# Softcap attention followed by a four-expert attention layer: stage B by two slots per token instead of four experts, its gate on GpSimd, and one exponential per pair of heads in stage A

## The chip, the cores and the metric

One NeuronCore of a Trainium2 chip runs the whole program. The metric is the device time of one execution in microseconds, the median over runs.

## The reference

`q`, `k` and `v` have shape (8, 12, 448, 64): batch, heads, tokens, head width. Stage A is attention with a soft cap, without a causal mask; stage B gives its output to an attention layer with E = 4 experts of width 64, of which each token uses the two with the largest gate logits.

```python
# stage A
scores = scale * np.matmul(q, k.transpose(0, 1, 3, 2))
scores = cap * np.tanh(scores / cap)
...
attn = np.exp(scores)
attn = attn / (np.sum(attn, axis=-1, keepdims=True) + 1e-09)
...
# stage B: x is stage A's output, (8, 448, 768)
logits = x @ w_gate
topk = np.argpartition(-logits, K, axis=-1)[..., :K]      # K = 2
...                                                       # w: softmax over the two chosen logits
for e in range(E):
    q = x @ wq[e]; k = x @ wk[e]; v = x @ wv[e]
    scores = scale * (q @ k.transpose(0, 2, 1))
    causal = np.triu(np.ones((S, S), dtype=bool), 1)
    ...                                                   # softmax, causal, in a
    ye = a @ v @ wo[e]
    for kk in range(K):
        mask = topk[:, :, kk] == e
        out += mask[..., None] * w[:, :, kk:kk + 1] * ye
```

In stage B every token is a key for every expert; only as a query does it belong to two of them.

## The kernel before, in words

**Stage A** goes over 48 pairs of heads (six pairs, HP, make one batch). GpSimd casts q, k and v of a pair to f16 four pairs ahead (`a_cast`, L241 to L263). TensorE transposes them into one PSUM tile (`a_tr`, L272 to L279), and VectorE copies them out (L289 to L296, L223). The scores of a pair are seven blocks of 128 keys by 448 queries, four for the first head and the tail of both, three for the second. `fill` (L305) computes them in four parts, T0 to T3, of 2, 2, 2 and 1 blocks, each into a tile of `ps_score`, a PSUM pool of two buffers. `tanh` (L318) reads each part on ScalarE; `expo` (L328) then takes the exponential of the first head's four blocks (1792 columns) and of the second's three (1344). `a_pv` (L337 to L369) multiplies with v on TensorE and normalizes on VectorE; `a_xt` (L383) transposes the result into `xT`, stage B's input, with six pairs per batch.

**Stage B** follows each batch while stage A goes on with the next one. `b_qk` (L486) and `b_v` (L395) project q, k, v and the logits from `xT`; two experts (index r, then e = 2r + g) share one 128-row tile of q and k. The k copy on VectorE spreads the two experts over separate columns with zeros in the other half (`b_k_out`, L479), so that `b_fill` (L516) gets one expert's scores, 1024 or 960 columns without the blocks above the diagonal. `b_exp` (L534) takes their exponential on ScalarE and GpSimd sets the diagonal blocks' upper parts to zero (L548). `b_gate` and `b_gate2` (L429, L449) find the two largest logits and their weights in nine small VectorE operations; `b_gexp` (L424) is the gate's exponential on ScalarE. `b_pv` (L553) multiplies with v for one expert and scales rows by weight over sum; `b_ot` (L582) and `b_wo` (L599) make the output. The last batch has no stage A beside it and goes its own way in `last_batch` (L798).

**Order.** The schedule is written by hand. `prog` (L688 to L697) fixes ScalarE's order: for a pair T0, T1, the second exponential of the pair before, T2, T3, the first exponential. In pairs 6(b+1)+3 and, as a rule, two later (`EXPB`, L685), the stage-B exponentials ("X") of batch b for r = 0 and r = 1 are put in, one before and one after the pair-before's exponential. A planner (`Plan`, L16 to L123) places TensorE's other work: each unit has an assumed TensorE and VectorE time, units that it needs, and a due time. `do_fill` (L714) first forces all that the next ScalarE tile needs (`fill_dep`, L711), then lets the planner emit other units until the score buffer is expected to be free, and then emits the fill. Engines run their queues in order, so a unit that waits holds back what is queued behind it. Four PSUM buffers (`ps_aux`) serve all else.

```python
            prog += t[0:2] + x[0:1] + e1 + x[1:2] + t[2:4] + [("E", p, 0)]
```

Of the kernel before, what the change touches and what calls it, by code (L numbers as in the profile page):

```python
# [125 lines left out]
def kernel(  # L126
# [26 lines left out]

    WIN = (0, 128, 256, S - 128)

    const = ctx.enter_context(tc.tile_pool(name="const", bufs=1))
# [158 lines left out]
    y = {}  # L315
    pr = {}

    def tanh(p, i):  # L318
        g = i // 2
        n = len(HALF[i])  # L320
        if i % 2 == 0:
            y[(p, g)] = actp.tile([128, 4 - g, S], f16, name=f"y{g}_{p}", tag=f"y{g}")
        nc.scalar.activation(  # L323
            y[(p, g)][:, 2 * (i % 2) : 2 * (i % 2) + n, :], score.pop((p, i))[:, 0:n, 0:S],
            AF.Tanh, scale=isc / capf,
        )

    def expo(p, g):  # L328
        pt = actp.tile([128, 4 - g, S], f16, name=f"p{g}_{p}", tag=f"p{g}")
        nc.scalar.activation(pt, y.pop((p, g)), AF.Exp, scale=capf)  # L330
        pr[(p, g)] = pt

# [4 lines left out]
    def a_pv_mm(p, i, n, heads):  # L337

        if n == 0 and 0 in heads:
            pvs[p, i] = ps_aux.tile([128, 2, 2, Dh + 1], f32, name=f"pv{i}_{p}", tag="aux")  # L340
        pv = pvs[p, i]
        w = WIN[2 * i + n]
        for g in heads:
            pt = pr[(p, g)]
            if g == 0:
                nc.tensor.matmul(  # L346
                    pv[:, n, :, :], pt[:, KC, w : w + 128], vtz[p % 8], start=(n == 0),
                    stop=False, skip_group_check=True,
                )
            for c in range(KC):  # L350
                nc.tensor.matmul(  # L351
                    pv[:, n, g, :], pt[:, c, w : w + 128], v16[p % 8][:, g, c, :],
                    start=False, stop=(c == KC - 1), skip_group_check=True,
                )

    def a_pv_out(p, i):
        pv = pvs.pop((p, i))
        if i == 0:
            xt[p] = hd.tile([128, 4, 2, Dh], f16, name=f"xk_{p}", tag="xk")
        else:  # L360
            del pr[(p, 0)], pr[(p, 1)]
        rc = hd.tile([128, 2, 2, 1], f32, name=f"rc{i}_{p}", tag="rc")
        nc.vector.reciprocal(rc, pv[:, :, :, Dh : Dh + 1])  # L363
        nc.vector.tensor_tensor(  # L364
            xt[p][:, 2 * i : 2 * i + 2, :, :], pv[:, :, :, 0:Dh],
            rc.broadcast_to((128, 2, 2, Dh)), ALU.mult,
        )
# [27 lines left out]
    def b_v(b, n, i):  # L395
        s = st[b]
        if n == 0 and i == 0:
            s["vall"] = bp.tile([128, KC, E, Dh + 1], f16, name=f"vall_{b}", tag="vall")
            s["lg"] = bp.tile([128, 4, E], f32, name=f"lg_{b}", tag="lg")
            nc.gpsimd.memset(s["vall"][:, :, :, Dh : Dh + 1], 1.0)  # L400
        w = WIN[n]
# [12 lines left out]
        if b < B - 1:  # L414
            nc.vector.tensor_copy(s["lg"][:, n, :], ps[:, E * Dh : E * Dh + E])
        if n < 3:
            evac(s["vall"][:, n, :, 0:Dh], pse, act=(b == B - 1 and n > 0))
        else:
            assert b < 2 or ("pvB", b - 2, E - 1) in plan.done
            vb = vtB[b % 2]  # L420
            nc.vector.tensor_copy(vb[0:64, 0:E:2, 0:Dh], pse[64:128, 0:E:2, :])
            nc.vector.tensor_copy(vb[64:128, 1:E:2, 0:Dh], pse[64:128, 1:E:2, :])
# [26 lines left out]
    def b_gate2(b):  # L449
# [14 lines left out]
        s["wtok"] = wtok  # L464

    def b_qk_mm(b, r, which, ps, j0, j1):
        w2 = wq2 if which == "q" else wk2
# [11 lines left out]
    def b_k_out(b, r, ps, act=False):  # L479
        assert b < 1 or ("X", b - 1, r, 1) in plan.done  # L480
        kk = kzB[r]
        nc.vector.tensor_copy(kk[0:64, 0:S], ps[0:64, :])
        nc.vector.tensor_copy(kk[64:128, S : S + TL], ps[64:128, KM:S])
        evac(kk[64:128, S + TL : 2 * S], ps[64:128, 0:KM], act)

    def b_qk(b, r, which, i):  # L486
# [4 lines left out]
        if i == 2:  # L491
            (b_q_out if which == "q" else b_k_out)(b, r, ps)

# [17 lines left out]

    COL = {(0, 0): 64, (0, 1): 512, (0, 2): 832, (1, 1): 1024, (1, 2): 1344, (1, 0): 1536}
# [19 lines left out]
    def b_exp(b, r, g):  # L534

        assert b < 2 or ("pvB", b - 2, E - 1) in plan.done
        pb = pB[2 * (b % 2) + r]
        n = 1024 - 64 * g
# [14 lines left out]
    def b_pv(b, e):  # L553

        s = st[b]
        r, g = divmod(e, 2)
        pb = pB[2 * (b % 2) + r]
        if g == 0:
            s["osc", r] = bp.tile([128, 4, 2, Dh], f16, name=f"osc_{b}_{r}", tag="osc")
        pv = ps_aux.tile([128, 4, Dh + 1], f32, name=f"pvB_{b}_{e}", tag="aux")  # L560
        for n in range(4):
# [5 lines left out]
            if n == 3:  # L567
                ops.append((0, vtB[b % 2][:, e, :]))
            for i, (o, rhs) in enumerate(ops):
# [83 lines left out]
    kzB = [const.tile([128, 2 * S], f16, name=f"kzB{i}") for i in range(2)]  # L653
    vtB = [const.tile([128, E, Dh + 1], f16, name=f"vtB{i}") for i in range(2)]
    pB = [const.tile([128, 64 + 1984], f16, name=f"pB{i}") for i in range(4)]

    def b_const(i):
        nc.vector.memset(kzB[i], 0.0)
        nc.vector.memset(vtB[i], 0.0)
        nc.vector.memset(vtB[i][0:64, 0:E:2, Dh : Dh + 1], 1.0)  # L660
        nc.vector.memset(vtB[i][64:128, 1:E:2, Dh : Dh + 1], 1.0)
        for t in pB[2 * i : 2 * i + 2]:
            nc.vector.memset(t[:, 0:64], 0.0)

# [19 lines left out]

    EXPB = {HP * (b + 1) + 3 + 2 * r - (b == B - 2) * r: (b, r) for b in range(B - 1) for r in range(2)}  # L685


    prog = []  # L688
    for p in range(NP):
        t = [("T", p, i) for i in range(4)]  # L690
        e1 = [("E", p - 1, 1)] if p else []
        x = [("X", *EXPB[p], g) for g in range(2)] if p in EXPB else []
        prog.append(("S", p))
        if p < NP - 1:
            prog += t[0:2] + x[0:1] + e1 + x[1:2] + t[2:4] + [("E", p, 0)]
        else:
            prog += t + e1 + [("S", NP), ("E", p, 0), ("E", p, 1)]  # L697
    reads = [o for o in prog if o[0] in "TX"]
# [5 lines left out]
    def dur(o):  # L704
        if o[0] == "S":
            return 0.0
        if o[0] == "X":
            return 0.9
        return 0.06 + 0.373 * (4 - o[2] if o[0] == "E" else len(HALF[o[2]]))

    def fill_dep(o):  # L711
        return (("tr", o[1]),) if o[0] == "T" else (("q", o[1], o[2]), ("k", o[1], o[2]))

    def do_fill():  # L714
# [8 lines left out]
        plan.pe = max(plan.pe, rel, *(plan.done[d] for d in fill_dep(o))) + cost  # L723
        fill(*o[1:]) if o[0] == "T" else b_fill(*o[1:])
        plan.done[("f", nfill)] = plan.pe + plan.LAT
# [11 lines left out]
    def slot(p):  # L737
# [14 lines left out]
        if 1 <= p < NP:  # L752
            es = [("E", p - 1, 0), ("E", p - 1, 1)]
            due = nom["S", p + 1]
# [18 lines left out]
    def batch(b):  # L773
        x = ("xt", HP * b + HP - 1)
        t0, t1 = nom["X", b, 0, 0], nom["X", b, 1, 0]
        pace = 1.0 if b < B - 2 else 0.3
        for r, t in enumerate((t0, t1)):
            plan.parts(("q", b, r), 3, 1.13, 0.55, [x], t - 4.0, b_qk, b, r, "q")
            plan.parts(("k", b, r), 3, 1.13, 0.75, [x], t - 4.0, b_qk, b, r, "k")
        for n in range(4):  # L780
            d = [("v", b, n - 1)] if n else [x]
            plan.parts(("v", b, n), 2, 0.66, 0.6, d, t0 + 2.0 * n, b_v, b, n)
        plan.add(("g1", b), 0.0, 1.0, [("v", b, 3)], t1 + 1.0, b_gate, b, aux=None)
        plan.add(("g", b), 0.0, 0.8, [("g1", b), ("G", b)], t1 + 3.0, b_gate2, b, aux=None)
        for e in range(E):
            due = t1 + pace * (6.0 + 3.0 * e)
            d = [("X", b, e // 2, e % 2), ("g", b)] + [("pvB", b, e - 1)] * (e % 2)
            plan.add(("pvB", b, e), 0.46, 0.7, d, due, b_pv, b, e)
            if e % 2:
                plan.add(("oT", b, e // 2), 0.22, 0.35, [("pvB", b, e)], due, b_ot, b, e // 2)  # L790
        for n in range(4):
            for f in range(2):
                i = 2 * n + f
                d = [("oT", b, 1)] if i == 0 else [("wo", b, *divmod(i - 1, 2))]
                due = t1 + pace * (19.0 + 1.5 * i)
                plan.add(("wo", b, n, f), 0.33, 0.5, d, due, b_wo, b, n, f)

# [98 lines left out]

    ngate = 0

    def gate_exp(wait=False):

        nonlocal ngate
        d = plan.done.get(("v", ngate, 3))
        if d is not None and (wait or d <= plan.act):
            b_gexp(ngate)
            plan.act = max(plan.act, d) + 0.1
            plan.done[("G", ngate)] = plan.act + plan.LAT
            ngate += 1

    nread = 0
    for pos, o in enumerate(prog, 1):  # L910
# [3 lines left out]
        if o[0] == "E":  # L914
            plan.act += dur(o)
            expo(*o[1:])
            plan.done[o] = plan.act + plan.LAT
            gate_exp()
            continue
# [6 lines left out]
        else:  # L926
            b_exp(*o[1:])
            gate_exp()
            plan.done[o] = start + dur(o) + plan.LAT + 0.6
# [41 lines left out]
```

The softmax here doesn't subtract the row's maximum and nothing guards it: scores larger than these inputs give would overflow.

## Time and profile before

| | |
|---|---|
| Median of 3 runs | 340.6 us (339.47, 340.60, 344.87) |
| Profiled execution: time, and span from first to last instruction | 341.0 us, 341.0 us |
| From 9.7 to 311.8 us (stage A, with stage B of seven batches) | ScalarE 298.0 us busy of 302.1, TensorE 257.1, VectorE 230.6, GpSimd 157.8 |
| From 311.8 us to the end (the last batch's stage B) | 29.2 us; ScalarE 8.1, TensorE 17.8 |
| Granted TensorE clock | 0.989 |

In the profile PE is TensorE, PEld its weight loads, DVE VectorE, ACT ScalarE, POOL GpSimd. A timeline line has the start and the duration in us, the engine, the source line, the operation, output and inputs by their names with shapes, and in brackets the idle time before it with what ended it. Names: `s` scores of stage A, `y` tanh, `p` its exponential, `pv` products with v, `xk` the normalized output, `tps` and `xtp` transposes, `qps`, `kps`, `vps` projections, `sB` and `pB` scores and exponential of stage B, `wops` and `ob` the output. Durations of consecutive instructions on one engine overlap.

### The profile page before, as it was taken

How to read it: one execution, taken by the hardware profiler on the slowest of the kernel's cores; microseconds unless marked ns; L12 is line 12 of the kernel's file. 1: busy time of each engine (PE TensorE's matmuls, PEld its weight loads, DVE VectorE, ACT ScalarE, POOL GpSimd, SP SyncE). 2: the span in 40 equal slices, each digit the busy share in tenths (PEclk: the TensorE clock that was granted, in tenths of full speed). 3: DMA queues.
4: the chain of work that ended last, by engine and by line, in shares of the span. 5: the costliest groups of instructions: out<-in, count | busy, mean ns of one | idle time of the engine just before them, and what ended most of it. 6: DMA issues, size and time to landing. Idle time of an engine off the chain costs nothing.

```text
span 341.0 us, 8954 instructions
## 1 busy us (share of the span) xinstructions
PE 280.2 (82%) x3295; PEld 190.1 (56%) x3295; DVE 251.1 (74%) x877; ACT 308.4 (90%) x341; POOL 165.2 (48%) x527
## 2 busy tenths in 40 slices
PE   5766669697899789998799879997899789979772
PEld 1344346465457565765576655765576566657441
DVE  2456656378767897869977897889887897788673
ACT  1999999689999999999999999999999999995422
POOL 2889999555806293256707291438506430220130
PEclk9999999799999999999999999999999999999997
DMA  5989999860172915392087606490162001210116
GB/s 160 264 222 244 244 223 241 202 173 3 48 208 72 293 32 171 123 289 71 7 253 211 184 2 187 138 303 24 47 210 72 3 2 46 94 24 2 48 54 226
DMA packets 65148, 46.21 MB, mean 136 GB/s; under 512 B 25872, under 2 KB 61584, under 8 KB 65104
## 3 DMA queue, kind: packets, MB, share of 16 engines
q1 hardware_dynamic: 53712, 43.43, 44.4%
q0 software_dynamic: 10512, 1.58, 7.3%
q10 hardware_dynamic: 880, 0.62, 0.6%
q8 instruction: 26, 0.43, 0.5%
q14 instruction: 18, 0.15, 0.1%
HBM read 36.19 MB, written 11.01 MB: 138 GB/s over the span
## 4 chain that ended last, share of the span: by engine, by line
ACT 85%; PE 6%; DMA 2%; issue 2%; DVE 2%; POOL 1%; ACTq 0%; POOLq 0%
ACT y L323 39%; ACT p L330 37%; ACT pB L540 7%; POOL pB L548 1%; DMA kf<-in_k_dram 1%; PE qkps L469 1%; PE vps L407 1%; PE s L312 1%; DMA out_dram<-ob 1%; PE sB L528 1%; DMA vtf<-in_v_dram 1%; DVE ob L223 1%; PE qps L469 0%; PE pv L351 0%; ACT L223 0%
## 5 line engine op out<-in xcount | busy, mean ns | idle before, releaser
L323 ACT ACTIVATE y<-s 128x896 f16<-128x896 f32 x192 | 152.6, 880 | 1.9 <-PE s L312 1.9
L330 ACT ACTIVATE p<-y 128x1792 f16<-128x1792 f16 x96 | 149.6, 1562 | 0.0
L548 POOL TENSOR_SCALAR_AFFINE_SELECT pB<-pB 128x128 f16<-128x128 f16 (+1 forms) x128 | 31.9, 280 | 142.9 <-ACT pB L540 141.7
L312 PE MATMUL s<-qt,kz 128*128 128x448 f16 x288 | 82.0, 357 | 14.0 <-ACT y L323 6.0
L351 PE MATMUL pv<-v,p 128*128 128x65 f16 x1152 | 66.2, 194 | 1.2 <-ACT p L330 1.0
L351 PEld LDWEIGHTS <-p 128*128 128x128 f16 x1152 | 53.7, 98 | 11.0 <-ACT p L330 2.0
L346 PE MATMUL pv<-vtz,p 128*128 128x130 f16 x192 | 42.0, 220 | 3.1 <-DVE kz L223 3.0
L364 DVE TENSOR_TENSOR xk<-pv,rc 128x256 f16<-128x256 f32 x96 | 40.7, 424 | 3.3
L312 PEld LDWEIGHTS <-kz 128*128 128x128 f16 x288 | 26.2, 98 | 26.4 <-issue 13.1
L223 DVE COPY ob<-wops 128x384 f32<-128x384 f32 (+1 forms) x60 | 33.1, 556 | 9.3 <-PE wops L594 8.5
L540 ACT ACTIVATE pB<-sB 128x1024 f16<-128x1024 f32 (+1 forms) x32 | 31.9, 999 | 2.4 <-PE sB L528 2.4
L223 DVE COPY kz<-tps 64x384 f16<-64x384 f16 x94 | 32.9, 350 | 0.7
L379 PE MATMUL xtp<-perm,xk 128*128 128x128 f16 x144 | 21.0, 223 | 14.4 <-DVE xk L364 14.2
L594 PE MATMUL wops<-wo,oT 128*128 128x384 f16 x128 | 29.8, 325 | 1.7 <-DVE oT L588 1.7
L407 PE MATMUL vps<-wvg,xT 128*128 128x260 f16 (+1 forms) x192 | 30.6, 276 | 0.0
L379 PEld LDWEIGHTS <-xk 128*128 128x128 f16 x192 | 14.6, 98 | 27.3 <-DVE xk L364 19.1
L363 DVE RECIPROCAL rc<-pv 128x4 f32<-128x4 f32 x96 | 17.2, 179 | 16.6 <-PE pv L351 15.4
L241 POOL CAST q<-qf 112x512 f16<-112x512 f32 x46 | 28.2, 613 | 2.0
L289 DVE COPY qt<-tps 128x384 f16<-128x384 f16 x48 | 16.9, 352 | 15.2 <-PE tps L279 14.8
L242 POOL CAST k<-kf 128x384 f16<-128x384 f32 x48 | 24.4, 509 | 5.0 <-DMA kf<-in_k_dram 5.0
L390 DVE COPY xT<-xtp 128x448 f16<-128x448 f16 x48 | 18.6, 388 | 11.2 <-PE xtp L379 10.8
L258 POOL CAST v<-vf 128x384 f16<-128x384 f32 x48 | 24.4, 508 | 3.5 <-DMA vf<-in_v_dram 0.5
(100 smaller groups left out, 500.5 us busy)
## 6 DMA issues: line engine op xcount, KB each, us to landing
qf<-in_q_dram SPq DMA_DIRECT2D x23, 448.0 KB, 5.2
out_dram<-ob SPq DMA_DIRECT2D x24, 384.0 KB, 2.8
kf<-in_k_dram SPq DMA_DIRECT2D x23, 384.0 KB, 5.3
vf<-in_v_dram SPq DMA_DIRECT2D x23, 384.0 KB, 4.6
ktf<-in_k_dram SPq DMA_DIRECT2D x46, 32.0 KB, 4.7
vtf<-in_v_dram SPq DMA_DIRECT2D x46, 32.0 KB, 4.1
out_dram<-ob SPq DMA_DIRECT2D x7, 192.0 KB, 2.8
qf<-in_q_dram ACTq DMA_DIRECT2D x2, 224.0 KB, 4.1
```

What stands on the lines that cost most here:

```text
L223: (nc.scalar.copy if act else nc.vector.tensor_copy)(dst, src)
L312: nc.tensor.matmul(sc[:, o, 0:S], lhsT, qt, start=True, stop=True)
L323: nc.scalar.activation(y[(p, g)][:, 2 * (i % 2) : 2 * (i % 2) + n, :], score.pop((p, i))[:, 0:n, 0:S], AF.Tanh, scale=isc / capf,)
L330: nc.scalar.activation(pt, y.pop((p, g)), AF.Exp, scale=capf)
L346: nc.tensor.matmul(pv[:, n, :, :], pt[:, KC, w : w + 128], vtz[p % 8], start=(n == 0), stop=False, skip_group_check=True,)
L351: nc.tensor.matmul(pv[:, n, g, :], pt[:, c, w : w + 128], v16[p % 8][:, g, c, :], start=False, stop=(c == KC - 1), skip_group_check=True,)
L364: nc.vector.tensor_tensor(xt[p][:, 2 * i : 2 * i + 2, :, :], pv[:, :, :, 0:Dh], rc.broadcast_to((128, 2, 2, Dh)), ALU.mult,)
L379: nc.tensor.transpose(ps[:, 128 * n : 128 * (n + 1)], src(n), first if n < 3 else last)
L407: nc.tensor.matmul(ps, xT[b][:, j, w : w + 128], wvg[:, j, 0:cols], start=(j == 0), stop=(j == NDC - 1),)
L540: nc.scalar.activation(pb[:, o0 : o0 + n], st[b].pop(("sc", r, g))[:, 0:n], AF.Exp, scale=isc)
L548: nc.gpsimd.affine_select(out=blk, in_=blk, compare_op=ALU.is_ge, fill=0.0, base=0, pattern=[[1, n]], channel_multiplier=-1,)
L594: nc.tensor.matmul(ps, st[b]["oT", r][:, w : w + 128], wo2[r][:, f * (D // 2) : (f + 1) * (D // 2)], start=(r == 0), stop=(r == 1),)
```

## The change

Stage B, for all batches but the last, no longer runs four experts but two slots a = 0, 1: a token's first and second chosen expert in the order of their indices. q of the experts that aren't in the slot is set to zero per token, and the scores of a slot are the sum over both 128-row tiles, so that each token meets its own expert's keys. Slot 0 can hold experts 0 to 2 and slot 1 experts 1 to 3; the product with v is made for the three experts at once, and rows are scaled per expert with weights that are zero for the others. There are thus two exponentials of 1024 columns per batch instead of four (two of 1024, two of 960), with a fill of eight matmuls each. The gate (`s_gate`) moves to GpSimd, with powers of e instead of ScalarE's exponential; it makes the masks, which TensorE transposes (`s_mask`). In stage A the two exponentials of a pair become one of 3136 columns (not in the last pair), and `prog` is T0, T1, X, the exponential of the pair before, T2, T3. The last batch keeps its way with four experts.

The diff, cut to its core:

```diff
-    def expo(p, g):
-        pt = actp.tile([128, 4 - g, S], f16, name=f"p{g}_{p}", tag=f"p{g}")
-        nc.scalar.activation(pt, y.pop((p, g)), AF.Exp, scale=capf)
-        pr[(p, g)] = pt
+    def expo(p, k0, k1):
+
+        if k0 == 0:
+            pr[p] = actp.tile([128, 7, S], f16, name=f"p_{p}", tag="p")
+        nc.scalar.activation(
+            pr[p][:, k0:k1, :], y[p][:, k0:k1, :], AF.Exp, scale=capf
+        )
...
+    def s_gate(b):
...
+        ee = t("ee", E)
+        g.tensor_tensor(ee, euler, lg, ALU.pow)
+        df, gt = t("df", E, E), t("gt", E, E)
+        g.tensor_tensor(df, lgj, lgi, ALU.subtract)
+        g.tensor_scalar(gt, df, 0.0, None, ALU.is_gt)
+        for i in range(1, E):
+            g.tensor_scalar(gt[:, :, i, 0:i], df[:, :, i, 0:i], 0.0, None, ALU.is_ge)
+        r2, rank = t("r2", E, 2), t("rank", E, 1)
+        g.tensor_tensor(r2, gt[:, :, :, 0:2], gt[:, :, :, 2:4], ALU.add)
+        g.tensor_tensor(rank, r2[:, :, :, 0:1], r2[:, :, :, 1:2], ALU.add)
+        sel = t("slt", E)
+        g.tensor_scalar(sel, rank.rearrange("p n e o -> p n (e o)"), 1.5, None, ALU.is_lt)
+
+        mk = t("mk", 8, 1, dt=f16)
+        g.memset(mk, 0.0)
...
+        for a in range(2):
+            s["mb", a] = t(f"mb{a}", E, Dh, dt=f16)
+            g.tensor_copy(s["mb", a], mk[:, :, a:8:2, :].broadcast_to((128, 4, E, Dh)))
+
+        g.tensor_tensor(ee, ee, sel, ALU.mult)
...
+        g.tensor_tensor(den, den, minus, ALU.pow)
...
+        plan.done[("G", b)] = plan.pe + 9.0
+
+    def s_mask(b, a):
...
+        ps = ps_aux.tile([128, 2, 512], f16, name=f"mps{a}_{b}", tag="aux")
+        for r in range(2):
+            transpose4(
+                ps[:, r, :],
+                lambda n: mb[:, n, 2 * r : 2 * r + 2, :].rearrange("p e d -> p (e d)"),
+                ident, swap,
+            )
+        qm = bp.tile([128, 2, S], f16, name=f"qm{a}_{b}", tag=f"qm{a}", bufs=1)
+        nc.vector.tensor_tensor(qm, s["qs"], ps[:, :, 0:S], ALU.mult)
...
+    def s_fill(b, a):
+        s = st[b]
+        ks, qm = s["ks"], s["qm", a]
+        sc = ps_score.tile([128, 1024], f32, name=f"sS{a}_{b}", tag="score")
+        for c in (KC, 0, 1, 2):
+            k0, q0 = (S - 128, KM) if c == KC else (128 * c, 128 * c)
+            o = 0 if c == KC else SCOL[c]
+            for r in range(2):
+                nc.tensor.matmul(
+                    sc[:, o : o + S - q0], ks[:, r, k0 : k0 + 128], qm[:, r, q0:S],
+                    start=(r == 0), stop=(r == 1),
+                )
...
-            prog += t[0:2] + x[0:1] + e1 + x[1:2] + t[2:4] + [("E", p, 0)]
+            prog += t[0:2] + x + e1 + t[2:4]
...
     def fill_dep(o):
-        return (("tr", o[1]),) if o[0] == "T" else (("q", o[1], o[2]), ("k", o[1], o[2]))
+        if o[0] == "T":
+            return (("tr", o[1]),)
+        return (("mk", *o[1:]), ("k", o[1], 0), ("k", o[1], 1))
...
     def batch(b):
         x = ("xt", HP * b + HP - 1)
...
+        for r in range(2):
+            plan.parts(("q", b, r), 3, 1.13, 0.62, [x], t0 - 6.0, b_qk, b, r, "q")
         for n in range(4):
             d = [("v", b, n - 1)] if n else [x]
-            plan.parts(("v", b, n), 2, 0.66, 0.6, d, t0 + 2.0 * n, b_v, b, n)
...
+            plan.parts(("v", b, n), 2, 0.66, 0.6, d, t0 - 16.0 + 2.0 * n, b_v, b, n)
+        plan.add(("g", b), 0.0, 0.0, [("v", b, 3)], t0 - 14.0, s_gate, b, aux=None)
+        for r in range(2):
+            plan.parts(("k", b, r), 3, 1.13, 0.62, [x], t0 - 4.0, b_qk, b, r, "k")
+        for a, t in enumerate((t0, t1)):
+            d = [("G", b), ("g", b), ("q", b, 0), ("q", b, 1)]
+            plan.add(("mk", b, a), 0.5, 1.05, d, t - 4.0, s_mask, b, a)
```

New, too: `s_exp` (the exponential and four selects on GpSimd for a slot), `s_pv` (20 products of 193 columns per batch, with three VectorE operations for each of four token windows), `s_ot`, and plain copies of k (`s_k_out`: one of 448 columns per r instead of three).

## The prediction

> **What bounds the kernel now.** I read the page's engine shares and chain first, then ScalarE's timeline around one stage-B insertion, then TensorE, VectorE and GpSimd in the same window.
>
> ```profile
> PE 280.2 (82%) x3295; PEld 190.1 (56%) x3295; DVE 251.1 (74%) x877; ACT 308.4 (90%) x341; POOL 165.2 (48%) x527
> ...
> ACT 85%; PE 6%; DMA 2%; issue 2%; DVE 2%; POOL 1%; ACTq 0%; POOLq 0%
> ACT y L323 39%; ACT p L330 37%; ACT pB L540 7%; POOL pB L548 1%; DMA kf<-in_k_dram 1%; PE qkps L469 1%; PE vps L407 1%; PE s L312 1%; DMA out_dram<-ob 1%; PE sB L528 1%; DMA vtf<-in_v_dram 1%; DVE ob L223 1%; PE qps L469 0%; PE pv L351 0%; ACT L223 0%
> ```
>
> ScalarE is 90% busy and is 85% of the chain: the span is the sum of its starts. Its timeline (columns: start us, us, engine, line):
>
> ```profile
> 147.27 0.95 ACT L323 ACTIVATE y<-s 128x896 f16<-128x896 f32 x1
> 148.07 1.36 ACT L330 ACTIVATE p<-y 128x1344 f16<-128x1344 f16 x1
> 149.28 0.25 ACT L427 ACTIVATE eexp<-lg 128x16 f32<-128x16 f32 x1
> 149.39 1.39 ACT L323 ACTIVATE y<-s 128x896 f16<-128x896 f32 x2
> 150.61 1.75 ACT L330 ACTIVATE p<-y 128x1792 f16<-128x1792 f16 x1
> 152.20 1.78 ACT L323 ACTIVATE y<-s 128x896 f16<-128x896 f32 x2
> 153.91 1.02 ACT L540 ACTIVATE pB<-sB 128x1024 f16<-128x1024 f32 x1
> 154.83 1.31 ACT L330 ACTIVATE p<-y 128x1344 f16<-128x1344 f16 x1
> 156.05 0.96 ACT L540 ACTIVATE pB<-sB 128x960 f16<-128x960 f32 x1
> 156.90 1.35 ACT L323 ACTIVATE y<-s 128x896 f16<-128x896 f32 x2
> ```
>
> Durations overlap; the cost is start to start: tanh of 896 columns 0.80 (lasts 0.95), of 448 1.22 - 0.80 = 0.42, exponentials 1.21 (1344) and 1.59 (1792), stage B 0.92 and 0.85, gate 0.11. Before 153.91 there are 1.71 for two tanh worth 1.60: 0.11 of waiting. TensorE, VectorE and GpSimd there:
>
> ```profile
> 153.22 0.19 PE L522 MATMUL sB<-qe,kzB 128*128 128x64 f16 x1 [0.24 <-ACT y L323]
> 153.25 0.57 PE L528 MATMUL sB<-qe,kzB 128*128 128x448 f16 x3
> ...
> 154.48 0.36 DVE L289 COPY qt<-tps 128x384 f16<-128x384 f16 x1
> ...
> 155.73 0.18 DVE L363 RECIPROCAL rc<-pv 128x4 f32<-128x4 f32 x1
> 155.95 0.42 DVE L364 TENSOR_TENSOR xk<-pv,rc 128x256 f16<-128x256 f32 x1
> 156.29 0.35 DVE L289 COPY qt<-tps 128x384 f16<-128x384 f16 x1
> ...
> 157.87 0.61 POOL L241 CAST q<-qf 112x512 f16<-112x512 f32 x1
> 158.43 0.51 POOL L242 CAST k<-kf 128x384 f16<-128x384 f32 x1
> 158.88 0.53 POOL L245 CAST ktz<-ktf 64x64 f16<-64x64 f32 x2
> ```
>
> This gives the price of a score buffer: the tanh that frees it ends at 153.17 (start + about 0.95), the fill starts 0.05 later, four matmuls of 1024 columns end at 153.82, ScalarE starts at 153.91.
>
> **The skill.** "ScalarE: Activation LUTs", What ACT_TABLE_LOAD costs: 186 ns + 0.833 per element, back-to-back ones overlapping by 93 ns, so about 93 ns + 0.833 per element between starts. The trace agrees: 1792 x 0.833 = 1493, + 93 = 1.59. "GPSIMD Engine Reference", Specifications: GpSimd cannot access PSUM; so a gate there can only begin after VectorE has copied the logits. No run yet shows arithmetic on two tensors there; the same page, Performance versus the Vector engine, gives 4497 ns for 2048 fp32, hence my estimate of 0.14 us plus overhead for 64.
>
> **What it takes off ScalarE.** One exponential of 3136 costs 2.61 + 0.09 = 2.71 for 2.80: 0.09 x 47 = 4.4 us. Per batch two stage-B exponentials of 1024 instead of two of 1024 and two of 960: 14 x 0.85 = 11.9. Seven gate exponentials at 0.11: 0.7. Together 17.0.
>
> **What it adds, 1: the order of tanh.** Before, an exponential stood between the tanh pairs, so every fill had 1.6 us or more of cover. Now T2, T3 and the next pair's T0, T1 are adjacent, and there are two score buffers. T0's fill waits for T2's end: T2's start + 0.93 (its duration) + 0.05 + 0.54 (two matmuls of 448 columns, from start to end in TensorE's timeline) + 0.04 = 1.56, while ScalarE wants it at 0.80 + 0.42 = 1.22. Wait 0.34 per pair, at 46 boundaries 15.6; at the first the transposes of pair 1 are late as well, 1.6. Bounds 0.3 (the shortest path) to 0.5 (TensorE late): 14 to 23.
>
> **What it adds, 2: the second exponential of a batch.** Its fill is 8 matmuls, 2048 columns, 1.02 instead of 0.60, with one tanh as cover: 0.95 + 0.05 + 1.02 + 0.04 - 1.61 = 0.43. Seven times 3.0; the present waits there (14 of 0.14 on average) go: -2.0.
>
> **What it adds, 3: the first exponential of a batch.** This decides. The changed kernel's own instruction order says what is queued where. The place is still pair 6(b+1)+3, after its two tanh, but before it needed q and k of experts 0 and 1 alone; now its fill needs q and k of all, all logits, the gate on GpSimd, the transposed mask and the masked q. In TensorE's queue, for each of batches 1 to 6, these stand between that pair's T1 fill and the stage-B fill: vps_1 to vps_3, qps_1, both kps, six pv groups, two pairs' transposes, five output products, two xtp. T1's fill cannot start before the previous pair's T3 ends (same buffer). Take that as zero; ScalarE then wants stage B at 1.80 (T0 from 0.20, T1 from 1.00).
>
> TensorE, from starts in its timeline (448 columns 0.188, a v product 0.11, a pv group of seven 0.25): 0.05 + T1's fill 0.37 + 18 q/k matmuls 3.38, less four that follow (0.75), + 15 v matmuls 1.65 + two pv 0.50 + xtp 0.22 = 5.4. The last logits land at 5.6.
>
> VectorE then has, in its queue ahead of the mask product: logits and v 0.5, two k copies (448) 1.1, two pv evacuations 1.1 (0.22 + 0.34 each), two pairs' transposes 2.4 (1.25 each above, a little less unhindered), one xT 0.3, four output copies 1.9 and a 64-row one 0.6: 7.9, so to 13.5. TensorE alone would be at the mask's transposes at 5.4 + 0.75 + four pv 1.0 + five output products 1.6 + 0.84 + xtp 0.22 = 9.8.
>
> GpSimd: 13 small dependent operations to the mask. The ktz casts run 0.27 to 0.3 apart; I take 0.3, so 3.9, plus 1.2 extra for the power (which no row shows; bounds 0 to 6), plus the 1024-element spread 0.96 (512 and 384 elements take 0.55 and 0.45 from start to start: 0.15 + 0.79 ns each). From 5.8 to 11.9: just inside VectorE's 13.5.
>
> Then the mask product, 896 columns from PSUM, 1.05 (256 take 0.34, 448 take 0.54), the fill 1.02 and 0.1 of hand-overs: ScalarE starts at 15.7. Wait 13.9. Batch 0 has no outputs and one transposed pair less in front: GpSimd decides, 13.0. Sum 6 x 13.9 + 13.0 = 96.4. Bounds: 10.8 (TensorE alone) to 17.4 (each small GpSimd operation 0.5, the power 3).
>
> **At nothing.** TensorE per batch: 16 transposes more (0.9), value products 20 of 193 columns (1.6) for 40 of 65 (1.2), the same score columns; VectorE about 0.8 less (ten gate operations 1.7 and three-part k copies fewer, two mask products of 1.05 more). They lie beside ScalarE, except those counted above; uncovered, they would cost 0.5 a batch. GpSimd gets some 24 operations per batch for 8 affine selects, about 7 us net in 38 at 48% busy; casts are made four pairs ahead, so a cast 7 us late still comes in time. Later stage-B products wait for GpSimd's selects (0.25 each, four) with 3.5 us until the next T0 fill. The probability buffers: three, and pv of three pairs earlier stands before the need in TensorE's queue. No DMA moves past another. Tail (29.2 us after the last exponential) is kept.
>
> **Sum**, against the profiled execution's 341.0 (the median of the runs, 340.6, is 0.4 away): 341.0 - 17.0 + 15.6 + 1.6 + 3.0 - 2.0 + 96.4 - 2.5 (a one-time wait of batch 0 at 62 us that the longer one swallows) = 436.
>
> **Rivals.** *GpSimd's chain ends last by far.* From logits to mask over 7.7 us, it passes VectorE. With 0.5 per operation and a power of 3 it gives 436 + 7 x 3.5 = 460; with a power of 6, near 480. For: unseen operations on the critical path. Against: small GpSimd work above runs at 0.3.
> *Stage B is ready in time* (not slower). It needs everything before the mask off TensorE's queue within about 1 us of T1's fill, so one place, the first stage-B fill; then only the 0.34s remain: 436 - 96.4 = 340. For: nothing else is so large. Against: the queue shows 40 groups there, with data dependences.
> *Half the wait*: outputs and transposes overlap better than in my serial sum, and all chains shrink to about 7: 436 - 49 = 387.
> *The plain reading*: no waits at all, 341 - 17 = 324, VectorE and TensorE still under ScalarE. It needs a third score buffer, which isn't there.
>
> **Chances.** Forecast 0.68 (its own range 414 to 452), GpSimd last 0.18, half 0.07, in time 0.05, plain 0.02. The range 405 to 472 leaves out the last two, most of the half case and GpSimd's far end. Within 2% is about what a measurement can tell from no change: faster 0.02, same 0.04, slower 0.94.
>
> **What would show it.** The page: ScalarE's share down to about 68%, with its stage-B line at x14 plus the last batch's four; the chain a mix, with stage B's mask product and the GpSimd gate in it. ScalarE's timeline: one gap of 12 to 15 us before the first exponential of each batch, 0.4 before the second, 0.3 before each T0. If VectorE's outputs rather than GpSimd end the wait, the mask transposes on TensorE start right after the output products, without a wait for GpSimd. I am wrong if the seven gaps are below 9 us or above 18, or if T0 isn't delayed.

## The result and the profile after

| | before | after |
|---|---|---|
| Median, same chip, 4 runs each | 341.2 us | 453.5 us (451.79 to 454.67) |
| Profiled execution: time, span | 341.0, 341.0 us | 451.8, 450.1 us |
| Granted TensorE clock | 0.989 | 0.893 |

The changed kernel takes 1.331 times as long, 95% interval 1.326 to 1.337. Page of the changed kernel, engine shares, chain by engine, and two groups (busy us and mean ns, then idle time of ScalarE before them):

```profile
PE 327.7 (73%) x3281; PEld 219.4 (49%) x3281; DVE 241.8 (54%) x794; ACT 297.1 (66%) x273; POOL 228.6 (51%) x634
...
ACT 49%; PE 26%; DVE 12%; POOL 4%; issue 4%; DMA 3%; SPq 1%; ACTq 0%; POOLq 0%
...
L324 ACT ACTIVATE y<-s 128x896 f16<-128x896 f32 x192 | 147.7, 824 | 17.2 <-PE s L314 17.2
...
L623 ACT ACTIVATE pS<-sS 128x1024 f16<-128x1024 f32 x14 | 14.3, 1024 | 107.5 <-PE sS L613 107.5
```

ScalarE has less to do than before (297.1 for 308.4 us) and is now idle for a third of the span, 153.0 us. Of this, 107.5 us stand in one row: before the fourteen stage-B exponentials. Its timeline around batch 4 (two tanh in one line are an `x2`):

```profile
270.83 2.82 ACT L333 ACTIVATE p<-y 128x3136 f16<-128x3136 f16 x1
273.53 1.35 ACT L324 ACTIVATE y<-s 128x896 f16<-128x896 f32 x2
275.14 1.73 ACT L324 ACTIVATE y<-s 128x896 f16<-128x896 f32 x2 [0.25 <-PE s L314]
291.62 1.02 ACT L623 ACTIVATE pS<-sS 128x1024 f16<-128x1024 f32 x1 [14.75 <-PE sS L613]
```

The first exponential of 3136 costs 273.53 - 270.83 = 2.70 from start to start. Then T2 and T3, T0 and T1 with a small hole between, and the large one. What ended it, in the timelines of the other engines there:

```profile
280.86 2.92 POOL L493 TENSOR_TENSOR ee<-euler,lg 128x16 f32<-128x16 f32 x1 [9.40 <-DVE lg L425]
...
287.08 2.02 POOL L513 COPY mb<-mk 128x1024 f16<-128x1024 f16 x2
...
287.59 1.15 DVE L225 COPY ob<-wops 128x384 f32<-128x384 f32 x2
288.95 0.62 DVE L541 TENSOR_TENSOR qm<-qs,mps 128x896 f16<-128x896 f16 x1 [0.21 <-PE mps L385]
...
289.63 1.89 PE L613 MATMUL sS<-qm,ks 128*128 128x64 f16 x8 [0.72 <-DVE qm L541]
```

Read it from below: the fill takes 1.89 us and starts after the mask product. The product starts 0.21 us after VectorE's last output copies, when the mask's transposes end on TensorE. The mask itself (the first of the two spreads) is done at 288.1 on GpSimd, whose chain began with a power of 2.92 us at 280.86, directly after the last logits. So GpSimd's and VectorE's queues end almost together.

I count ScalarE's waits from start to start, each start less the usual distance after the instruction before it; this is a little more than the profile's idle time, since a late tanh also loses its overlap. "First wait" and "second wait" are those before a batch's first and second stage-B exponential, and "T0 wait" is that before the T0 of a pair. The seven first stage-B exponentials wait 15.2, 15.4, 15.2, 13.9, 14.9, 15.4 and 15.1 us (105.0), the seven second ones 0.43 to 0.49 and 1.32 (4.2), the 47 T0 22.7. The work saved is 17.0, as forecast, and the waits of before that go are 4.5 (stage B) and 1.6 (tanh): 341.0 - 17.0 - 4.5 - 1.6 + 105.0 + 4.2 + 22.7 = 449.8, against a span of 450.1. So the whole difference is these three kinds of waits.

Times and ratios of the experiments are of executions in the faster of two states; only the profile of stage A's part with tanh cut 2, 2, 1, 2 is of a slower execution (383.2 us, some 4 more than the fast ones), so its waits are somewhat too high in sum.

### The profile page after: what moved, and what is told of

The parts are those of the page before. It is cut to its first block, busy times and chain, and to the rows that moved or that the text cites. A ratio compares the mean times of both kernels' runs of the same rounds, so it can differ in the third digit from the quotient of the medians.

```text
span 450.1 us, 8908 instructions
## 1 busy us (share of the span) xinstructions
PE 327.7 (73%) x3281; PEld 219.4 (49%) x3281; DVE 241.8 (54%) x794; ACT 297.1 (66%) x273; POOL 228.6 (51%) x634
## 4 chain that ended last, share of the span: by engine, by line
ACT 49%; PE 26%; DVE 12%; POOL 4%; issue 4%; DMA 3%; SPq 1%; ACTq 0%; POOLq 0%
ACT p L333 25%; ACT y L324 20%; PE s L314 7%; PE sS L613 5%; ACT pS L623 3%; PE vps L417 3%; DVE ob L225 3%; PE kps L547 2%; PE qps L547 2%; DVE kz L225 2%; DVE ks L573 2%; PE mps L385 1%; DMA vf<-in_v_dram 1%; PE pv L357 1%; DMA kf<-in_k_dram 1%
## 5 line engine op out<-in xcount | busy, mean ns | idle before, releaser
L324 ACT ACTIVATE y<-s 128x896 f16<-128x896 f32 x192 | 147.7, 824 | 17.2 <-PE s L314 17.2
L314 PE MATMUL s<-qt,kz 128*128 128x448 f16 x288 | 94.2, 407 | 70.4 <-ACT y L324 67.1
L333 ACT ACTIVATE p<-y 128x3136 f16<-128x3136 f16 (+2 forms) x49 | 135.2, 2763 | 0.0
L623 ACT ACTIVATE pS<-sS 128x1024 f16<-128x1024 f32 x14 | 14.3, 1024 | 107.5 <-PE sS L613 107.5
L314 PEld LDWEIGHTS <-kz 128*128 128x128 f16 x288 | 29.7, 108 | 86.2 <-issue 76.9
L357 PE MATMUL pv<-v,p 128*128 128x65 f16 x1152 | 69.5, 201 | 0.0
L357 PEld LDWEIGHTS <-p 128*128 128x128 f16 x1152 | 58.5, 104 | 12.0 <-issue 5.4
L493 POOL TENSOR_TENSOR ee<-euler,lg 128x16 f32<-128x16 f32 x7 | 20.5, 2923 | 62.5 <-DVE lg L425 62.5
L626 POOL TENSOR_SCALAR_AFFINE_SELECT pS<-pS 128x128 f16<-128x128 f16 (+1 forms) x56 | 14.4, 279 | 58.9 <-ACT pS L623 57.9
L225 DVE COPY kz<-tps 64x384 f16<-64x384 f16 x94 | 32.9, 350 | 0.7
L385 PE MATMUL xtp<-perm,xk 128*128 128x128 f16 x144 | 19.3, 223 | 17.2 <-DVE xk L370 12.7
L666 POOL TENSOR_TENSOR o<-o 128x512 f16<-128x512 f16 x7 | 8.0, 1150 | 42.4 <-DVE rc L369 42.4
L385 PEld LDWEIGHTS <-xk 128*128 128x128 f16 x192 | 14.1, 98 | 27.9 <-DVE xk L370 16.1
```

The source lines that it names most:

```text
L225: (nc.scalar.copy if act else nc.vector.tensor_copy)(dst, src)
L314: nc.tensor.matmul(sc[:, o, 0:S], lhsT, qt, start=True, stop=True)
L324: nc.scalar.activation(y[p][:, 2 * i : 2 * i + n, :], score.pop((p, i))[:, 0:n, 0:S], AF.Tanh, scale=isc / capf,)
L333: nc.scalar.activation(pr[p][:, k0:k1, :], y[p][:, k0:k1, :], AF.Exp, scale=capf)
L357: nc.tensor.matmul(pv[:, n, g, :], pt[:, c, w : w + 128], v16[p % 8][:, g, c, :], start=False, stop=(c == KC - 1), skip_group_check=True,)
L385: nc.tensor.transpose(ps[:, 128 * n : 128 * (n + 1)], src(n), first if n < 3 else last)
```

## The experiments

Ratios are to the kernel before on the same chip, with 95% intervals; waits are counted from start to start as above.

**Stage B's exponentials one pair later** (batches 0 to 5).

```diff
-    EXPB = {HP * (b + 1) + 3 + 2 * a - (b == B - 2) * a: (b, a) ...}
+    EXPB = {HP * (b + 1) + (3 + a if b == B - 2 else 4 + a): (b, a) ...}
```

> The changed kernel with its two stage-B exponentials of batches 0 to 5 moved one pair later (pairs 4 and 5 after the batch's end instead of 3 and 5; the last of the seven stays). Theory: the planner's due times move with the place, so that in TensorE's queue twelve q products, the last v products, all k products, two pairs' transposes and the outputs still stand between T1's fill and the stage-B fill; the first wait falls only from 15 to about 12 us in six batches: 436 us. Rival, that only the place matters: 5.9 us more of head start come off each of six waits: 417 us.

441.6 us, 1.298 (1.292 to 1.304). First waits 9.2, 13.5, 13.9, 13.1, 13.4, 13.9, 14.7 (91.7 in all), while second waits grow from about 0.5 to between 1.1 and 1.3. A whole pair of more room takes off only 1 to 2 us per batch but for the first: due times are counted back from the place, so most of the work moves along with it. The theory is nearer than the rival, though the gain is smaller than it said.

**Tanh cut 2, 2, 1, 2**, so that the part before the next T0 has two blocks and covers its fill (offsets and the planner's times are changed to match).

```diff
-    HALF = (((0, 0), (0, 1)), ((0, 2), (0, 3)), ((1, 0), (1, 1)), ((1, 2),))
+    HALF = (((0, 0), (0, 1)), ((0, 2), (0, 3)), ((1, 0),), ((1, 1), (1, 2)))
```

> The changed kernel with the four parts of a pair cut 2, 2, 1, 2 blocks instead of 2, 2, 2, 1. Theory: T2 now ends early and T3 gives T0's fill 0.80 us of cover where 0.78 is needed, so the 47 waits before T0 (22.8 us in the sum) nearly vanish, and the seven long waits become some 2 us shorter, since a little more of stage B is queued ahead of T1's fill: 421 us, 430 if only the T0 waits go. Rival, that TensorE's lateness or its half clock and not the buffer's cover makes the T0 waits: less than 8 us gained, 446 us or more.

431.6 us, 1.268 (1.262 to 1.273). ScalarE's timeline of that kernel, batch 4:

```profile
261.89 2.83 ACT L334 ACTIVATE p<-y 128x3136 f16<-128x3136 f16 x1
264.60 2.99 ACT L325 ACTIVATE y<-s 128x448 f16<-128x448 f32 x4
280.55 1.02 ACT L624 ACTIVATE pS<-sS 128x1024 f16<-128x1024 f32 x1 [12.96 <-POOL wm L524]
```

T2, T3, T0, T1 run as one block of four without the hole: the T0 waits are 10.7 instead of 22.7, 8.6 of this at three places early in stage A (T1 waits 3.1 more). First waits are 13.0 to 14.8 (94.2 in all instead of 105.0), so about half of the gain is theirs. (The line names a GpSimd step as releaser; TensorE's fill ends within 0.02 us of it, and it is the fill that ends the wait of the thirteen other stage-B exponentials.)

**The power behind the masks** on GpSimd, since only the weights need it.

```diff
-        ee = t("ee", E)
-        g.tensor_tensor(ee, euler, lg, ALU.pow)
...
             g.tensor_copy(s["mb", a], mk[:, :, a:8:2, :].broadcast_to((128, 4, E, Dh)))
+        ee = t("ee", E)
+        g.tensor_tensor(ee, euler, lg, ALU.pow)
```

> The changed kernel with the first power on GpSimd (2.9 us each) moved behind the masks in GpSimd's queue, nothing else. Theory: GpSimd and VectorE reach the mask product almost together in batches 1 to 6, so taking 2.9 us off GpSimd alone gives 0.3 us or less there and the whole 2.9 only in batch 0, where VectorE has less queued: 449 us. Rival, GpSimd's chain alone ends the wait: 7 x 2.9 = 20 us less, 433 us.

445.3 us, 1.308 (1.304 to 1.312). The other engines' timelines of that kernel, batch 4:

```profile
280.37 2.01 POOL L511 COPY mb<-mk 128x1024 f16<-128x1024 f16 x2
...
283.80 1.15 DVE L225 COPY ob<-wops 128x384 f32<-128x384 f32 x2
284.98 0.62 DVE L541 TENSOR_TENSOR qm<-qs,mps 128x896 f16<-128x896 f16 x1
...
285.66 1.05 PE L613 MATMUL sS<-qm,ks 128*128 128x64 f16 x8 [1.13 <-DVE qm L541]
```

The masks are 2.9 us earlier, at 10.3 instead of 13.2 after the end of the previous T3, and yet the mask product starts at 13.89 instead of 14.06, because VectorE's output copies end at 13.86. So GpSimd's chain alone was not what held batch 4. Most of the gain of 8 us comes from elsewhere: the mask's transposes and the fill now run at full clock in four of seven batches (the fill takes 1.05 instead of 1.89 us there), and batch 0, where VectorE has less queued, gains 1.8.

**Mask work ahead**: the power behind the masks, and the planner takes the gate as ready at once, so it queues the mask's transposes earlier on TensorE.

```diff
-        plan.done[("G", b)] = plan.pe + 9.0
+        plan.done[("G", b)] = plan.pe
```

> As the kernel with the power moved behind the masks, and the planner is told that the gate takes no time, so that it queues the mask's transposes right behind the projections and not behind the outputs, transposes and value products of other pairs. Theory: with both chains shorter (mask at 9.9 us after the release, then the remaining k products and the fill at half clock) the first wait falls from 15 to about 12.4 us: 435 us, less gain if the work that no longer fits into the wait delays later fills. Rival, that only VectorE's queue counts: the wait falls to about 9, 411 us.

438.3 us, 1.287 (1.282 to 1.293). In batches 2 to 6 the mask product now ends at about 11.8, but the fill starts only at 13 to 14: the k products and their copies, which now stand between the two, have become the last. First waits 12.2 to 14.7. The cause taken away uncovers the next within 1 to 2 us, and the gain is near the theory's, not the rival's.

**Stage B's part alone**: stage A with two exponentials per pair in their old order.

> The changed kernel with stage A's two exponentials per pair in their old places (T0, T1, stage B, second exponential of the pair before, T2, T3, first exponential), that is, stage B's part of the change alone. Theory: ScalarE works 4.4 us more, the waits before T0 (22.8 us in the sum) go, and the first stage-B wait of a batch falls from 15 to about 13.5, since a little more of stage B is queued before: 428 us. Rival, that the new ScalarE order starves TensorE of time and thereby makes the long waits: they fall to half, 380 us.

419.5 us, 1.234 (1.228 to 1.239). First waits 10.5 to 12.8 (82.5), less than the theory's 13.5 but far from half. Without the merge VectorE is done sooner (12.4) and the mask's chain (11.8, and its transposes to 12.5) ends almost with it.

**Stage A's part alone**: the kernel before, with one exponential per pair and its order.

> The kernel before with one exponential per pair in stage A and its ScalarE order, nothing of stage B's change. Theory: 4.4 us less on ScalarE and the waits before T0 more, 47 of 0.38 and a few longer ones, 18 to 23 us: 356 us. Rival, that merging is what it says and the waits come from stage B: 337 us.

382.5 us, 1.124 (1.120 to 1.128): far more than either theory gave. T0 waits are 21.1, about what was expected; in addition ScalarE waits 26.6 us before stage B with its four experts. Timelines of that kernel, batch 4, second half:

```profile
251.95 0.55 DVE L223 CAST kzB<-kps 64x384 f16<-64x384 f32 x1
...
252.09 0.20 PE L526 MATMUL sB<-qe,kzB 128*128 128x64 f16 x1 [1.17 <-DVE kzB L487]
...
252.80 1.02 ACT L544 ACTIVATE pB<-sB 128x1024 f16<-128x1024 f32 x1 [3.28 <-PE sB L532]
```

The k products stand directly before the fill on TensorE, before both halves of all seven batches, and their copies end last on VectorE. In the kernel before, two of stage A's fills (once four), or at least 1.2 us of other products, lay between them.

**The same with tanh cut 2, 2, 1, 2.**

> As the kernel before with one exponential per pair, and the parts of a pair cut 2, 2, 1, 2 instead of 2, 2, 2, 1. Theory: T3 now covers T0's fill, the waits before T0 fall under 0.05 each, and the 4.4 us of the merge are kept: 337 us, faster than the kernel before. Rival, that TensorE, busy 85% of that stretch, loses the stretches it needs for stage B when fills come back to back: 345 us or more.

380.7 us, 1.117 (1.111 to 1.122). T0 waits are 6.1, as meant, but the waits before stage B rise to 32.9 (4.1 to 4.6 for most second halves) and those of the other tanh to 8.8. What one gives, the other takes; the rival was nearer.

**Stage B's part alone, four pairs later**, at pairs 6(b+1)+7 and +8, with earlier due times and the power behind the masks (batch 6 stays, as the pairs end).

```diff
-    EXPB = {HP * (b + 1) + 3 + 2 * a - (b == B - 2) * a: (b, a) ...}
+    EXPB = {HP * (b + 1) + ((3, 4) if b == B - 2 else (7, 8))[a]: (b, a) ...}
...
-            plan.parts(("v", b, n), 2, 0.66, 0.6, d, t0 - 16.0 + 2.0 * n, b_v, b, n)
+            plan.parts(("v", b, n), 2, 0.66, 0.6, d, t0 - 22.0 + 2.0 * n, b_v, b, n)
```

> The changed kernel with stage A's exponentials again two per pair in their old order, the power moved behind the masks, and the two stage-B exponentials of batches 0 to 5 at pairs 6(b+1)+7 and +8 with v due 6 us, q 8 us and k 10 us earlier; only batch 6 keeps pairs +3 and +4. The work of stage B is that of the run with two exponentials (419.5 us), only its place differs. By the instruction order twelve stage-A fills now lie between a batch's last logits and its stage-B fill (over 17 us), instead of none, and about 1.2 us of TensorE's work between the preceding fill and it. Theory (place and due times make the waits, not the amount of work): the first waits of batches 0 to 5 fall from about 12 to under 1, batch 6 keeps 11 to 14; ScalarE's own work is 341.0 - 11.9 - 0.7 = 328.4, less 4.5 of present stage-B waits, plus 2 for second fills, 13 for batch 6 and some 4 at the head: 342 us (range 335 to 352). Rival (GpSimd's gate, VectorE's mask products and TensorE's extra transposes take time that the other work of these engines needs, so waits come back elsewhere): still over 375 us.

366.5 us, 1.075 (1.069 to 1.081). First waits of batches 0 to 5 are 0.5 to 0.9 us instead of 10.5 to 12.8, so the place, with the due times that go with it, had made them. Batch 6, left in place, waits 16.9. The expected 342 is missed by 20 us in the profile (362.5): tanh of stage A waits 15.6, where 4 were counted, batch 6 waits 3.9 more than its 13, and the six small first waits, 4.0 in all, were counted as nothing. One of the waits before tanh, 4.6 us, in GpSimd's and TensorE's timelines of that kernel:

```profile
111.74 2.94 POOL L514 TENSOR_TENSOR ee<-euler,lg 128x16 f32<-128x16 f32 x1
...
117.35 1.15 POOL L666 TENSOR_TENSOR o<-o 128x512 f16<-128x512 f16 x1
...
118.55 0.50 PE L385 MATMUL otS<-ident,o 128*128 128x128 f16 x3 [5.05 <-POOL o L666]
```

TensorE, whose queue holds the next fill behind this transpose, waits for an addition of stage B's output on GpSimd, which stands there behind the next batch's gate.

**The whole change, later**, with both remedies: cut 2, 2, 1, 2, power late, pairs +6 and +8.

> The changed kernel whole, with its single exponential per pair, but tanh cut 2,2,1,2 instead of 2,2,2,1, the power behind the masks, the stage-B exponentials of batches 0 to 5 at pairs 6(b+1)+6 and +8, with v due 4, q 2 and k 6 us earlier. By the instruction order seven fills lie between the last logits and the stage-B fill, and 0.7 or 3.6 us (in turn) of TensorE's work directly before it. Theory: T0 waits near nothing but for some 8 us in the first twelve pairs, first waits 0 to 4 us (about 12 in all) and 14 for batch 6, second ones 0.4: 341.0 - 17.0 + 8 + 12 + 14 + 3 = 361 us (range 352 to 375). Rival (one exponential per pair leaves TensorE and VectorE too few stretches for the rest of their work, whatever the place of stage B): 390 us or more.

381.3 us, 1.119 (1.114 to 1.125), between the theory and the rival. First waits 3.9, 1.7, 8.4, 1.8, 8.4, 1.8, 16.5. Timelines at batch 2, one of those of 8.4:

```profile
169.38 1.15 POOL L667 TENSOR_TENSOR o<-o 128x512 f16<-128x512 f16 x1
...
170.59 0.34 PE L386 MATMUL otS<-ident,o 128*128 128x128 f16 x3 [2.54 <-POOL o L667]
...
174.83 1.02 ACT L624 ACTIVATE pS<-sS 128x1024 f16<-128x1024 f32 x1 [8.27 <-PE sS L614]
```

Again the addition of the batch before, behind the gate's powers and the casts on GpSimd, holds TensorE up, here with the mask transposes of batch 2 behind it. A further 9.6 us at T0 of pair 9 has TensorE waiting for the first batch's k weights from memory, which land at 67.5 us, 20.4 after their transfer was issued.

**Stage A's part alone, stage B later** (pairs +5 and +7, due times of q and k 10 us earlier).

> The kernel before with stage A's single exponential per pair only (382.5 us), and the two halves of stage B at pairs 6(b+1)+5 and +7 instead of +3 and +5, with q and k due 10 us earlier; batch 6 keeps +3 and +4. In the run without this shift ScalarE waits 26.6 us in all before the first exponential of each half, nine of them over 0.7 us, because the last copy of k on VectorE ends after TensorE's fill could start; in the new order at least two fills lie between the last k product and every stage-B fill but those of batch 6. Theory (again the place): these waits fall to 7 us, nothing else changes: 382.5 - 20 = 363 us (range 357 to 369), the T0 waits of about 0.4 per pair remain. Rival (TensorE has too few stretches between the adjacent fills, so the same waits appear elsewhere): 376 us or more.

369.1 us, 1.084 (1.079 to 1.088). This order never reached the gate of batch 6, so that batch's value products, weights and output products are left out. Repeated with the due times of batch 6 as they were, which computes all:

> As the run before with one exponential per pair and stage B at pairs +5 and +7, except that q and k of batch 6 keep their due times. (In that run the planner never came to the gate of batch 6, so its value products, weights and output products were left out, of one batch in eight; here all is computed.) Theory (the place makes the stage-B waits): the waits of batches 0 to 5 stay under 0.3 us each, batch 6 has about 5, as there, and its output work is hidden beside ScalarE or in the tail: 369 to 374 us, against 382.5 with the old places. Rival (the left-out work had made the gain): 380 us or more.

375.3 us, 1.103 (1.098 to 1.108). The waits before stage B fall from 26.6 to 9.9, as the place theory wants (batch 6 has nearly all of these), but T0 waits grow from 21.1 to 30.1. In the one of 1.6 us at 302.3, the T0 fill waits on TensorE for VectorE's late copy of that pair's transposes:

```profile
301.41 0.74 PE L312 MATMUL s<-qt,kz 128*128 128x448 f16 x3 [0.99 <-DVE kz L223]
```

Net 7.7, measured 7.2. The rival is half right: there is not room for everything.

**The gate on VectorE** (first power still on GpSimd, second one as a reciprocal).

```diff
-        g = nc.gpsimd
+        g = nc.vector
```

> The changed kernel with the gate's small operations on VectorE instead of GpSimd (only the first power stays on GpSimd, the second becomes VectorE's reciprocal); order and due times unchanged. About 20 small operations and two spreads of 1024 elements per batch move into VectorE's queue, ahead of the transposes, output copies and the mask product that stand there now. Theory (VectorE's queue, which ends 13.9 us after the previous pair's last tanh, sets the mask product as much as GpSimd's mask at 13.2): some 13 x 0.2 + 2 x 0.6 + 6 x 0.15 = 4.7 us later per batch, less 1 of VectorE's idle time: first waits 18 to 19 us instead of 15, 453.5 + 7 x 3.7 = 479 us (range 465 to 490). Rival (GpSimd's slow small operations alone make the wait): the mask is ready 4 us earlier and the waits fall to 12: about 432 us.

482.7 us, 1.419 (1.411 to 1.427). VectorE's and ScalarE's timelines of that kernel, batch 3:

```profile
245.99 1.30 DVE L513 COPY mb<-mk 128x1024 f16<-128x1024 f16 x2
...
255.62 0.62 DVE L541 TENSOR_TENSOR qm<-qs,mps 128x896 f16<-128x896 f16 x1 [0.29 <-PE mps L385]
...
258.29 1.02 ACT L623 ACTIVATE pS<-sS 128x1024 f16<-128x1024 f32 x1 [19.72 <-PE sS L613]
```

The masks are ready 8.3 us before the product, which stands behind VectorE's transposes and output copies; these start 4.4 us later for the gate. First waits 19.8 to 20.6. GpSimd was not the cause of the wait; with the gate there, it is shorter.

## Why the prediction was right, and where its sizes were off

The mechanism, its place and the sign held: ScalarE has less to do, and waits of some 15 us before each batch's first stage-B exponential cost far more. 450.1 is 14 above 436. It lies within the forecast's own range, 414 to 452; the median of the runs, 453.5, lies just above that. By its steps, in us:

- *What it takes off ScalarE*, 17.0: right. 2.70 per exponential of 3136 (forecast 2.71), 14 stage-B exponentials at 0.92.
- *The order of tanh*, 17.2: measured 22.7. A T0 waits 0.38, not 0.34, at most places, 0.66 to 0.75 at six where TensorE runs at half clock, and 3.0 at the first two for 1.6. The cut 2, 2, 1, 2 leaves 2.1 of it outside three early places, so the cause is shown.
- *The second exponential*, 0.43 each (the terms as written add to 0.45): right (0.43 to 0.49), but for 1.32 in batch 6, whose fill ran at half clock.
- *The first exponential*, 96.4: measured 105.0. The scale is the prediction's own, from the end of the previous T3. Value products end at 5.6 (forecast 5.6), VectorE's queue at 13.9, in two batches at 14.3 (13.5), the masks at 13.2 (11.9); the mask product takes 0.62 (1.05). The exponential starts at 15.76 in batch 3 (15.7) but at 16.7 to 17.3 in the others. The step mis-sized is the fill: 1.02 in the sum, 1.89 in six of seven batches, at half clock. The transposes of the mask, 0.6 to 1.1, were not in the sum of batches 1 to 6, where the mask was to be ready well before VectorE; the shorter product paid for about half of them.
- *Which queue ends last*: called for VectorE, and it is all but a tie. The masks come later than forecast, since the power takes 2.92 where 1.2 was added, and their transposes end 0.04 to 0.43 after VectorE's queue in batches 1 to 6. The forecast sign held in four of these six: TensorE starts the transposes right after the output products. In the other two it starts 0.29 later, when the mask and one of VectorE's output copies end almost together. In batch 0 TensorE waits 3.2 for the mask, as forecast. With the masks 2.9 earlier the product of batch 4 starts only 0.17 earlier, and with the gate on VectorE all is later. That the dear power cost so little is luck: VectorE's queue happened to be as long as the slower chain.
- *At nothing*: right. The three terms above add 8.6 + 5.5 + 1.2 = 15.3 to 436, the waits of before that go are 6.1 and not 4.5, and the span is 14.1 above, so nothing else of size is left. The tail takes 29.2 as before.

Of the rivals, *GpSimd last by far* has its premise (a dear power) but not its consequence, since VectorE ends with it. *Ready in time* and *half the wait* need another place: with stage B later they come about for six batches. *The plain reading* was right about ScalarE's work and wrong in that its inputs would be there. Each part of the change alone brings such waits: the two cost 79 and 42 us, together 113.

What I hadn't seen is the second half of stage A's part. With one long exponential in place of two shorter ones the planner puts stage B's k products directly before their use even with four experts, which cost about 22 us there (26.6 for 4.5). That the place of these products makes the waits is shown, as moving it took 17 us of them away. Why the planner chose that place is only argued: TensorE has fewer stretches between adjacent fills, but its value products now also wait for the whole pair's exponential, and no run separates the two. In the whole change this is contained in the chain counted from the order of instructions, so the sum came out without it.

Still open is whether a better order would bring the change under the kernel before. No version here does: 366.5 is the lowest with two slots. Its profile, 362.5, has 16.9 of waiting in batch 6 and 15.6 before tanh; without these it would be near 330, an estimate from these numbers, and not tried. That order has two exponentials per pair in stage A; with one, none tried that computes everything came under 375.

## What to carry to other kernels

Less work on the busiest engine is worth something only if its inputs arrive: when a change lengthens the chain of dependent work to a fixed place in an order, move the place first and count what each queue holds between the last input and it. After each cause is removed, look at which queue is next: here GpSimd's masks, VectorE's copies and TensorE's k products each took over within 2 us, so no single remedy that kept the whole change was worth more than 22 of 113 us. Two instructions merged into one may also take away a place where other engines' work could be slipped in, so try such a merge alone first.

## What the runs showed of the hardware

The half clock was not expected. The window view of the changed kernel (us, then busy us and counts of PE, PEld, DVE, ACT, POOL, granted clock, DMA share, GB/s), in two windows and, finer, where the clock falls:

```profile
286.00:289.00 3.00, 1.77 (x16) 0.90 (x14) 2.73 (x8) 0.00 (x0) 2.77 (x7) 0.92 0.33 131
289.00:292.00 3.00, 2.37 (x10) 1.30 (x11) 0.57 (x1) 0.39 (x1) 2.32 (x8) 0.50 0.33 131
...
288.00:288.50 0.50, 0.33 (x6) 0.33 (x7) 0.47 (x2) 0.00 (x0) 0.50 (x2) 1.00 0.40 154
288.50:289.00 0.50, 0.41 (x6) 0.14 (x3) 0.29 (x2) 0.00 (x0) 0.50 (x1) 0.53 0.00 0
```

And the fill of batch 3 from its timeline:

```profile
237.75 1.05 PE L613 MATMUL sS<-qm,ks 128*128 128x64 f16 x8 [0.72 <-DVE qm L541]
```

The same eight matmuls take 1.05 at full and 1.89 at half clock. The Trainium skill, "TensorE: Matmul & The Clock Gate", Part 1: The HAM clock gate, says that the clock falls to half after an idle window of about 3.4 us. Here it fell just after 288.5 though TensorE had no gap above 0.85 us from 285.0 to 288.5; it had been busy for 1.6 of these 3.5 us, so a thin load was enough.

The fourteen traces show how thin, leaving out the first 15 and the last 4 us of each. The clock changes only at multiples of 3.41 us from one another; this length agrees with the page. Take the share of such a step in which the profile has TensorE busy. At full clock, all 104 steps below 43% were followed by half clock and none of the 1019 above 61%; of the 230 between, 33 were. At half clock, all 128 steps above 84% were followed by full clock and none of the 36 below 77%. So in this case a low busy share is enough before the clock halves, and an idle step is not needed. With the power moved, four of seven fills ran at full clock, where one of seven had.

A power costs GpSimd 2.92 us for 16 values per row and 1.04 for 4. The gate's steps from differences to masks take it 5.3 us (283.76 to 289.05) and VectorE, in the last experiment, 3.2 (243.99 to 247.20). VectorE multiplies 896 f16 values from SBUF and PSUM in 0.62 us.
